# Where w1, w2, one scratch quarter and the kept keys and values stand in the arena of a two-layer decode kernel

## The chip, the core and the metric

The kernel runs on one core of one Trainium2 chip. The metric is device microseconds of that core, from one launch that does everything. A core has a matrix engine (PE, with its weight loads shown apart as PEld), a vector engine (DVE), an activation engine (ACT), a general one (POOL) and SyncE (SP), which here does nothing but start transfers from memory. Sixteen DMA engines carry them.

## The reference

One token of 512 numbers goes through attention and MLP, and then through the same attention and the same MLP once more, with the same weights and the same caches:

```python
def _A_ref(x, k_cache, v_cache, wq, wo):     # x is 1x1x512, H = 32 heads of 128, 4096 cached positions
    q = (x @ wq).reshape(B, Sq, H, Dh) ...
    scores = einsum("bhqd,bhkd->bhqk", q, k_cache) * Dh ** -0.5
    o = einsum("bhqk,bhkd->bhqd", softmax(scores), v_cache)
    return o.reshape(B, Sq, H * Dh) @ wo
def _B_ref(x, w1, b1, w2, b2):               # F = 1376
    return gelu(x @ w1 + b1) @ w2 + b2
x = x + _A_ref(_layernorm(x), ...)
x = x + _B_ref(_layernorm(x), ...)
x = x + _A_ref(_layernorm(x), ...)
x = x + _B_ref(_layernorm(x), ...)
```

Everything is float32. Each cache is 67 MB, so each pass of attention has 134 MB to read.

## The kernel before

**Groups and quarters.** The 32 heads are taken in 8 groups of 4. A group's keys are one load of 8.39 MB (128 partitions of 16384 numbers), its values another. The unit of room is a quarter, U = 512 numbers in each partition (0.26 MB); 32 quarters hold one K or one V. For a group, 32 products with K give the scores in PSUM bank pS (`scores`, L190), `exponentials` (L195) writes the weights p into a scratch quarter of SBUF with an activation, four transposing products (`weights`, L206) bring p into the form that the 32 products with V want (`values`, L220, bank pO), and `head_out` (L225) turns the sum into a scratch quarter, reduces it to o and multiplies it with wo. The next group's query comes after that (`next_queries`).

**The arena.** SBUF is one tile of 109 quarters, and all loads go to fixed places in it. Three homes of 32 quarters stand one behind the other: A from 0, C from 32, B from 64 to 96. K and V of the groups go round in the order A, B, C (`RING`), so that in the first pass B receives V of group 0, K of group 2, V of group 3, K of group 5 and V of group 6 (called V0, K2, V3, K5, V6 below). From 101 stands PAIR, 8 quarters for a pair of weights wo and wq (2.1 MB). Between them the kernel has rooms with names: `SHARED` from 90 (10 quarters, behind the 26 of V6 that stay in B), and `SCRATCH`, the one quarter at 100, which is written twice in each group: by the activation with p, and by `head_out`.

**The second pass** takes the groups in the reverse order, n = 0 to 7 for groups 7 to 0. It finds K7 and V7 still in C and A, and V6 kept: 26 quarters in B and 6 in the PSUM banks pK, copied there by ACT and copied back later. From n = 2 on it loads again, K and V into A, C, B in turn: K(3), V(4), K(6) and V(7) go to B. V(2) is loaded in two pieces of 5 and 3 chunks (a chunk is 4 quarters), as C comes free.

**The change of layers.** Between the passes w1 (4 pieces of 2.69 quarters) and w2 (11 quarters) come through SHARED and the scratch quarter: w1 whole first, then w2 in four pieces into the room of the pieces of w1 that have been used, then wq and the first quarters of K6. Wide products with zeros (`idle`, L154) are put in between; they compute nothing that is used.

**What sets the order.** Each engine takes its instructions in the order in which the program wrote them, and `keep_in_program_order` holds loads and products to it. The framework gives an instruction a wait for every earlier one that reads or writes the same part of a tile. All loads are issued by SP (L70), in one queue: a load that waits holds those behind it. Loads of K and V are written into the program as far ahead as the homes allow.

Of the kernel before, what the change touches and what calls it, by code (L numbers as in the profile page):

```python
# [33 lines left out]


RING = (0, 16 * NC, 8 * NC)
A_AT, B_AT, C_AT = RING
KEPT_V = 26 * U
SHARED = B_AT + KEPT_V
SCRATCH = SHARED + 10 * U  # L40
PAIR = SHARED + 11 * U
ARENA = PAIR + 2 * NC
HALVES = ((0, 4), (4, 8))
W1_AT_END = ((0, 2), (2, 3), (3, 4))
LAST = ((0, 4), (4, 6), (6, 7), (7, 8))
W2_AT_CHANGE = ((0, 2), (2, 5), (5, 8), (8, 11))
W2_AT_END = ((0, 4), (4, 8), (8, 10), (10, 11))
# [3 lines left out]
def decode_layers(ctx: ExitStack, tc: tile.TileContext, x, k, v, w, w1, b1, w2, b2, out):  # L51
# [102 lines left out]
    def idle(to, n=U):  # L154
        matmul(to[:, :n], zero[:, 0:1].to_broadcast([P, P]), at(C_AT, n), start=True, stop=True)

    def minus_mean(s, at):
        for j in range(J):
            matmul(at[32 * j : 32 * j + 32, :], negmean, s, start=True, stop=True)
        return at  # L160

    def mean_of(xs, s):
        nm = minus_mean(s, pS[:, 0:1])
# [6 lines left out]
    def rstd_of(ss):  # L170
        nv = minus_mean(ss, pS[:, 1:2])
        ve, r = small("ve"), small("rstd")
        nc.vector.tensor_scalar(ve, nv, -1.0, EPS, op0=ALU.mult, op1=ALU.add)
        nc.vector.memset(pS[:, 0:2], 0.0)
        nc.gpsimd.tensor_tensor(r, ve, power, op=ALU.pow)
        return r
# [47 lines left out]

    def head_out(rl, wt, last=False):  # L225
        ot = at(SCRATCH, U)
        nc.vector.transpose(ot, pO)  # L227
        o, on = small("o", 4), on_wide
        own = at(SCRATCH, 4 * 129).rearrange("p (b q) -> p b q", q=129)[:, :, :P]
        own = own.rearrange("p b (d q) -> p d b q", q=32)[:, :, :, 0]  # L230
        nc.vector.tensor_reduce(o, own, axis=AX.X, op=ALU.add)  # L231
# [12 lines left out]
        return of_32(turned(pS) if last else turned(pO, wide=True), 4)  # L244

    def mlp(xs, s, w1_t, w2_t, load_w2=None):
        xb = small("xb", 4)
        nc.gpsimd.tensor_tensor(xb, pairs(xs)[:, :, 0], b2c, op=ALU.add)  # L248
        for c in range(4):
            for j in range(J):  # L250
                matmul(pO[32 * j : 32 * j + 2, :FJ], pairs(xs)[:, c, :], w1_t[c][:, FJ * j : FJ * (j + 1)],
                       start=(c == 0), stop=(c == 3))
# [60 lines left out]
    def add_up(acc, own):  # L313
        t = small("acc", 4)
        nc.vector.scalar_tensor_tensor(t, own, 1.0, acc, op0=ALU.mult, op1=ALU.add)
        return t


    negm, z, sc, nsc = first_queries(xs, s, wq_t)
    acc = pairs(xs)[:, :, 0]  # L320
    for g in range(G):
        final = g == G - 1
        k_home, v_home = RING[2 * g % 3], RING[(2 * g + 1) % 3]
        for c, t in blocks(k, g, k_home, HALVES if final else ((0, C),)):
            scores(z, c, t)
        pt, rl = weights(exponentials(sc, nsc))
        for c, t in blocks(v, g, v_home, LAST if final else ((0, C),)):
            values(c, pt, t, c)
            if final and c > 4:
                idle(pS)  # L330
            if g == G - 2:
                for j in range(J):
                    i = 4 * c + j - KEPT_V // U
                    if i >= 0:
                        nc.scalar.copy(pK[i], t[j])
        if final:
            wo_t = by_four(load(PAIR, of_w(g % 2, g, 1)))
            for i in range(3):
                load_w1(SHARED, i, i + 1)
            own = head_out(rl, wo_t, last=True)  # L340
            load_w1(SHARED, 3, 4)
        else:
            pair = load(PAIR, of_w(g % 2, g, 2))
            acc = add_up(acc, head_out(rl, by_four(pair[:, :NC])))
            wq_t = by_four(pair[:, NC:])
            z = next_queries(g + 1, xs, negm, wq_t)
    x1, s1 = set_x(own, 1.0, acc, queries=False)
    own, xb = mlp(x1, s1, in_rows(SHARED, W1C, 4), in_rows(SHARED, U, FB),
                  lambda i: load_w2(SHARED, *W2_AT_CHANGE[i]))
    xs, s = set_x(own, 0.5, xb)  # L350
# [6 lines left out]
    acc = pairs(xs)[:, :, 0]  # L357
    wq_t = by_four(load(SHARED, of_w((g + 1) % 2, g, 1)))
    k_t = []
# [5 lines left out]

    begin_k(SHARED + NC, 4)
    begin_k(SHARED + 2 * NC, 2)
    begin_k(PAIR + NC, 4)
    for c in range(C):
# [12 lines left out]

    v_t = [at(B_AT + U * i, U) for i in range(KEPT_V // U)]
    for i, first in enumerate([C_AT + 30 * U, C_AT + 31 * U] + [PAIR + U * j for j in range(4)]):
        t = at(first, U)
        nc.scalar.copy(t, pK[i])
        v_t.append(t)
    for c in range(C):
# [8 lines left out]
    for n in range(2, G):  # L397
# [67 lines left out]
```

## Time and profile before

| | before |
|---|---|
| median of 3 runs | 680.82 us (680.7 to 681.85) |
| the profiled execution | 679.55 us |
| its span, first to last instruction | 677.8 us |
| busy: PE, DVE, ACT | 433.1, 110.7, 22.2 us |
| granted TensorE clock, mean | 0.841 |
| read from HBM | 286.14 MB, 422 GB/s over the span |
| loads of SP, share of 16 DMA engines' span | 98.7% |

Times in the profile are microseconds from the span's start. A row of the timeline gives start, length, engine, line, operation, tiles, how many instructions were merged, and in brackets the idle time of the engine ahead of it with what ended it. Durations below are from this one execution; its time is 1.27 us under the median of the runs.

### The profile page before, as it was taken

To read this page: it belongs to the slowest core of one execution; us is meant where nothing else is said; L and a number is where in the kernel's file an instruction comes from. 1 tells how busy PE (TensorE), PEld (TensorE's weight loads), DVE (VectorE), ACT (ScalarE), POOL (GpSimd) and SP (SyncE) were. 2 spreads that over 40 slices of the span, in tenths; PEclk is the share of its full clock that TensorE was granted. 3 is DMA by queue.
4 is the path that set the end of the run, shared out by engine and by line. 5 is a ranking of instruction groups with operands and counts; after the bars stand their busy time and mean duration, and the time that the engine had idled before them with its cause. 6 is when DMAs were issued, how large, how long until landed. Compare 5 with 4: busy or idle time off the path is not lost. (4 is left out here: it accounts for less than half of the span.)

```text
span 677.8 us, 6359 instructions
## 1 busy us (share of the span) xinstructions
PE 433.1 (64%) x2792; PEld 119.4 (18%) x2792; DVE 110.7 (16%) x431; ACT 22.2 (3%) x47; POOL 4.3 (1%) x21
## 2 busy tenths in 40 slices
PE   1547666485554874667777897686455764766776
PEld 0112112121111211111113222221111111211112
DVE  1012101111021101210212312211021011210211
ACT  0010000000000000001000110000000000000000
POOL 1000000000000000000000000000000000000000
PEclk9969768797698876977979998998698776977977
DMA  9999999999999999999999999899999999999997
GB/s 372 434 433 433 435 433 433 416 449 437 430 433 413 451 433 430 433 431 422 428 413 359 426 459 414 358 468 441 427 433 398 465 433 423 437 430 410 426 416 294
DMA packets 11404, 286.56 MB, mean 423 GB/s; under 512 B 1776, under 2 KB 1776, under 8 KB 3440
## 3 DMA queue, kind: packets, MB, share of 16 engines
q1 hardware_dynamic: 10944, 286.14, 98.7%
q8 instruction: 22, 0.36, 0.2%
q10 hardware_dynamic: 432, 0.01, 0.0%
q14 instruction: 6, 0.05, 0.0%
HBM read 286.14 MB, written 0.00 MB: 422 GB/s over the span
## 5 line engine op out<-in xcount | busy, mean ns | idle before, releaser
L74 PE MATMUL pO<-arena,turned 128*4 128x512 f32 x1024 | 144.8, 726 | 76.8 <-DMA arena<-in_v 75.6
L74 PE MATMUL pS<-arena,zq 128*8 128x512 f32 x1024 | 137.7, 698 | 70.8 <-DMA arena<-in_k 65.4
L74 PE MATMUL pO<-arena,x_wide 128*128 128x512 f32 (+1 forms) x176 | 54.9, 508 | 24.4 <-DVE turned L137 18.1
L74 PE MATMUL pO<-arena,on_wide 128*128 128x512 f32 x112 | 51.8, 605 | 18.6 <-DVE on_wide L235 18.6
L74 PEld LDWEIGHTS pS<-arena,zq 128*8 128x8 f32 x1024 | 29.1, 99 | 176.3 <-issue 167.1
L74 PEld LDWEIGHTS pO<-arena,turned 128*4 128x4 f32 x1024 | 27.6, 97 | 183.8 <-issue 179.5
L137 DVE STREAM_TRANSPOSE turned<-pO 32x128 f32<-32x128 f32 x112 | 35.0, 312 | 101.1 <-PE pO L74 99.9
L227 DVE STREAM_TRANSPOSE arena<-pO 128x512 f32<-128x512 f32 x16 | 11.5, 717 | 220.4 <-PE pO L74 220.4
L208 PE MATMUL pO<-ident,arena 128*128 128x128 f32 x64 | 14.5, 368 | 43.9 <-ACT arena L203 42.4
L196 DVE TENSOR_REDUCE ml<-pS 128x1 f32<-128x512 f32 x16 | 11.1, 692 | 185.0 <-PE pS L74 185.0
L74 PEld LDWEIGHTS pO<-arena,x_wide 128*128 128x128 f32 (+1 forms) x176 | 21.6, 155 | 57.1 <-DVE turned L137 26.5
L203 ACT ACTIVATE arena<-pS,mt,sc 128x512 f32<-128x512 f32 x16 | 12.4, 777 | 523.7 <-DVE mt L201 523.7
L74 PEld LDWEIGHTS pO<-arena,on_wide 128*128 128x128 f32 x112 | 20.1, 189 | 51.7 <-DVE on_wide L235 31.6
L208 PEld LDWEIGHTS pO<-ident,arena 128*128 128x128 f32 x64 | 9.3, 181 | 58.6 <-ACT arena L203 51.3
L74 PE MATMUL pO<-arena,x 128*2 128x344 f32 x64 | 7.2, 531 | 5.0 <-DMA arena<-in_w 4.4
L74 PE MATMUL pS<-arena,zero 128*128 128x512 f32 x16 | 9.9, 706 | 0.0
L74 PE MATMUL pS<-arena,gelu_g 128*1 128x128 f32 x176 | 6.7, 290 | 1.5 <-DVE gelu_g L270 1.3
L213 DVE STREAM_TRANSPOSE mt<-ml 128x32 f32<-128x32 f32 x16 | 3.4, 212 | 17.2 <-ACT arena L203 17.2
L74 PEld LDWEIGHTS pS<-arena,gelu_g 128*1 128x1 f32 x176 | 3.9, 88 | 7.4 <-DVE gelu_g L270 3.7
L211 DVE COPY turned<-pO 128x128 f32<-128x128 f32 x16 | 4.4, 277 | 3.1 <-PE pO L208 3.1
L74 PE MATMUL pO<-arena,zero 128*128 128x512 f32 x8 | 4.5, 644 | 0.0
L248 POOL TENSOR_TENSOR xb<-x,b2c 128x4 f32<-128x4 f32 x2 | 0.4, 200 | 636.9 <-DVE x L148 636.9
(71 smaller groups left out, 76.5 us busy)
## 6 DMA issues: line engine op xcount, KB each, us to landing
arena<-in_w SPq DMA_DIRECT2D x13, 2048.0 KB, 28.8
arena<-in_k SPq DMA_DIRECT2D x4, 4096.0 KB, 42.5
arena<-in_v SPq DMA_DIRECT2D x2, 4096.0 KB, 47.6
arena<-in_w SPq DMA_DIRECT2D x6, 1024.0 KB, 20.3
arena<-in_v SPq DMA_DIRECT2D x1, 5120.0 KB, 23.8
arena<-in_w SPq DMA_DIRECT2D x6, 688.0 KB, 30.2
arena<-in_v SPq DMA_DIRECT2D x2, 2048.0 KB, 50.8
arena<-in_v SPq DMA_DIRECT2D x4, 1024.0 KB, 53.3
```

The costliest lines, as they stand in the source:

```text
L74: tc.keep_in_program_order(nc.tensor.matmul(*a, **kw))
L137: nc.vector.transpose(t[q], src[q, P * j : P * (j + 1)])
L196: nc.vector.tensor_reduce(ml[:, 0:1], pS, axis=AX.X, op=ALU.max)
L203: nc.scalar.activation(p, pS, AF.Exp, bias=bias[:, 0:1], scale=sc, accum_out=ml[:, 0:1])
L208: tc.keep_in_program_order(nc.tensor.transpose(pT[:, b].rearrange("p j r -> p (j r)"), p[:, P * b : P * (b + 1)], ident))
L211: nc.vector.tensor_copy(pt, pT[:, :, :, :C].rearrange("p b j c -> p j c b"))
L213: nc.vector.transpose(lt, ml)
L227: nc.vector.transpose(ot, pO)
L248: nc.gpsimd.tensor_tensor(xb, pairs(xs)[:, :, 0], b2c, op=ALU.add)
```

## The change

Constants first. V6 keeps 27 quarters in B and 5 in PSUM, and the PSUM bank that this frees takes the last quarter of K6, so the second pass reads 31 quarters of K6 instead of 32. SHARED begins at 91 and has 10 quarters. SCRATCH is moved from quarter 100 into that room: SHARED + 4 quarters, which is quarter 95. The last head output of the first pass has a place of its own (LAST_OT). w1's fourth piece goes into the first one's room once that is used, and w2 comes in five pieces (1, 2, 4, 3, 1 quarters).

In the MLP the products with w1 go to pS and the mean and variance to pO (before: the other way round), and idle products stand at other places. V(2) is loaded as 6 and 2 chunks.

```diff
 RING = (0, 16 * NC, 8 * NC)
 A_AT, B_AT, C_AT = RING
-KEPT_V = 26 * U
-SHARED = B_AT + KEPT_V
-SCRATCH = SHARED + 10 * U
-PAIR = SHARED + 11 * U
+KEPT_V, KEPT_K = 27, 1
+SHARED = B_AT + KEPT_V * U
+SCRATCH = SHARED + 4 * U
+LAST_OT = SHARED + 3 * W1C
+PAIR = SHARED + 10 * U
 ARENA = PAIR + 2 * NC
-W2_AT_CHANGE = ((0, 2), (2, 5), (5, 8), (8, 11))
+W1_AT_CHANGE = (0, W1C, 2 * W1C, 0)
+W2_AT_CHANGE = ((0, 1, 9 * U), (1, 3, 3 * U), (3, 7, 5 * U), (7, 10, 0), (10, 11, 3 * U))
...
+    def idle_beside(to, first):
+        matmul(to[:, first:], zero[:, 0:1].to_broadcast([P, P]), at(C_AT, U - first), start=False,
+               stop=False, skip_group_check=True)
...
-    def mlp(xs, s, w1_t, w2_t, load_w2=None):
+    def mlp(xs, s, w1_t, w2_t, load_w1=None, load_w2=None):
...
             if c == 0:
-                nm, ss = mean_of(xs, s)
+                nm, ss = mean_of(xs, s, pO)
+                if load_w1:
+                    load_w1(3)
             if c == 1:
-                r = rstd_of(ss)
-            if load_w2 and c < 3:
+                r = rstd_of(ss, pO)
+            if load_w2 and 0 < c < 3:
                 load_w2(c)
-        idle(pS)
-        ht = at(SCRATCH, 32 * FB)
-        nc.vector.transpose(ht, pO[:, : 32 * FB])
+                idle_beside(pS, 32 * FB)
+        ht = at(SHARED, 32 * FB)
+        nc.vector.transpose(ht, pS[:, : 32 * FB])
...
         if load_w2:
             load_w2(3)
+        idle(pS)
...
-            if load_w2 and any(c == b - 1 for a, b in W2_AT_CHANGE):
-                idle(pO)
+            if load_w2 and c == 1:
+                load_w2(4)
+            if load_w2 and c in (2, 6, 9, 10):
+                idle(pO, U if c < 4 else U // 2)
...
+        if g == G - 2:
+            for i in range(KEPT_K):
+                nc.scalar.copy(pK[4 * C - KEPT_V + i], t[J - KEPT_K + i])
...
-            for i in range(3):
-                load_w1(SHARED, i, i + 1)
-            own = head_out(rl, wo_t, last=True)
-            load_w1(SHARED, 3, 4)
+            for c in range(3):
+                w1_at_change(c)
+            own = head_out(rl, wo_t, last=True, place=LAST_OT)
+            w2_at_change(0)
+            idle(pO, U // 2)
...
-    begin_k(SHARED + NC, 4)
-    begin_k(SHARED + 2 * NC, 2)
+    begin_k(SHARED, 4)
+    begin_k(SHARED + 9 * U, 1)
     begin_k(PAIR + NC, 4)
...
-    pair = load(C_AT + 22 * U, of_w(g % 2, g - 1, 2))
+    pair = load(C_AT + 6 * NC, of_w(g % 2, g - 1, 2))
...
-        for c, t in blocks(v, g, v_home, LAST if final else ((0, 5), (5, 8)) if n == 2 else ((0, C),)):
+        for c, t in blocks(v, g, v_home, LAST if final else ((0, 6), (6, 8)) if n == 2 else ((0, C),)):
```

On SP's queue the loads of K and V stand in the same order as before. What each load waits for is not the same. The first loads of the first pass, before (K0, V0 into B, the first pair, K1, V1, the next pair, K2 into B; a name in brackets is a semaphore of the engine or of an earlier load):

```order
L70 DMA arena<-in_k 128x16384
L70 DMA arena<-in_v 128x16384 [waits DMAHW1_49,PE_49]
L70 DMA arena<-in_w 128x4096
L70 DMA arena<-in_k 128x16384
L70 DMA arena<-in_v 128x16384 [waits DMAHW4_49,DMAHW0_49,PE_49]
L70 DMA arena<-in_w 128x4096 [waits DMAHW6_49,PE_49]
L70 DMA arena<-in_k 128x16384 [waits DMAHW5_49,DMAHW2_49]
```

and the same loads after the change:

```order
L75 DMA arena<-in_k 128x16384
L75 DMA arena<-in_v 128x16384 [waits DMAHW1_49,PE_49,Activation_49]
L75 DMA arena<-in_w 128x4096
L75 DMA arena<-in_k 128x16384
L75 DMA arena<-in_v 128x16384 [waits DMAHW4_49,DMAHW0_49]
L75 DMA arena<-in_w 128x4096 [waits DMAHW6_49,PE_49]
L75 DMA arena<-in_k 128x16384 [waits DMAHW2_49,DMAHW5_49,DVE_49,PE_49]
```

V0 has a wait for ACT that it did not have, and K2 waits for DVE and PE that it did not have; V1, which goes to A, has lost its own wait for PE, which the one ahead of it in the queue now covers.

In the second pass, from the pair that precedes K(3): before,

```order
L70 DMA arena<-in_w 128x4096 [waits DMAHW3_49,Activation_49]
L70 DMA arena<-in_k 128x16384
L70 DMA arena<-in_v 128x16384 [waits DMAHW0_49,PE_49]
L70 DMA arena<-in_w 128x4096 [waits DMAHW3_49,PE_49]
L70 DMA arena<-in_k 128x16384 [waits DMAHW2_49,DMAHW1_49]
L70 DMA arena<-in_v 128x16384 [waits DMAHW4_49,PE_49]
```

and after the change:

```order
L75 DMA arena<-in_w 128x4096 [waits DMAHW4_49,Activation_49]
L75 DMA arena<-in_k 128x16384 [waits DVE_49,PE_49]
L75 DMA arena<-in_v 128x16384 [waits DMAHW1_49]
L75 DMA arena<-in_w 128x4096 [waits DMAHW4_49,PE_49]
L75 DMA arena<-in_k 128x16384 [waits DMAHW3_49,DMAHW2_49]
L75 DMA arena<-in_v 128x16384 [waits DMAHW5_49,PE_49,Activation_49]
```

K(3), the second row, had no wait at all and now waits for DVE and PE; V(4), the last row, waits for ACT besides.

More of the change, by code (lines that the diff above doesn't have):

```diff
@@ L160, in minus_mean, with mean_of @@
         return at
-    def mean_of(xs, s):
-        nm = minus_mean(s, pS[:, 0:1])
+    def mean_of(xs, s, bank=pS):
+        nm = minus_mean(s, bank[:, 0:1])
         xc, sq, ss, negm = small("xc", 4), small("sq", 4), small("ss"), small("negm")
@@ L168, in mean_of, with rstd_of @@
         return negm, ss
-    def rstd_of(ss):
-        nv = minus_mean(ss, pS[:, 1:2])
+    def rstd_of(ss, bank=pS):
+        nv = minus_mean(ss, bank[:, 1:2])
         ve, r = small("ve"), small("rstd")
         nc.vector.tensor_scalar(ve, nv, -1.0, EPS, op0=ALU.mult, op1=ALU.add)
-        nc.vector.memset(pS[:, 0:2], 0.0)
+        if bank is pS:
+            nc.vector.memset(pS[:, 0:2], 0.0)
         nc.gpsimd.tensor_tensor(r, ve, power, op=ALU.pow)
@@ L223, in values, with head_out @@
                    start=(i == 0), stop=(i == C - 1))
-    def head_out(rl, wt, last=False):
-        ot = at(SCRATCH, U)
+    def head_out(rl, wt, last=False, place=SCRATCH):
+        ot = at(place, U)
         nc.vector.transpose(ot, pO)
         o, on = small("o", 4), on_wide
-        own = at(SCRATCH, 4 * 129).rearrange("p (b q) -> p b q", q=129)[:, :, :P]
+        own = at(place, 4 * 129).rearrange("p (b q) -> p b q", q=129)[:, :, :P]
         own = own.rearrange("p b (d q) -> p d b q", q=32)[:, :, :, 0]
@@ L316, in add_up, with w1_at_change, w2_at_change @@
         return t
+    def w1_at_change(c):
+        load(SHARED + W1_AT_CHANGE[c], w1[:, W1C * c : W1C * (c + 1)])
+    def w2_at_change(i):
+        a, b, first = W2_AT_CHANGE[i]
+        load(SHARED + first, w2[:, U * a : U * b])
     negm, z, sc, nsc = first_queries(xs, s, wq_t)
@@ L332, in decode_layers @@
                 for j in range(J):
-                    i = 4 * c + j - KEPT_V // U
+                    i = 4 * c + j - KEPT_V
                     if i >= 0:
@@ L347, in decode_layers @@
     x1, s1 = set_x(own, 1.0, acc, queries=False)
-    own, xb = mlp(x1, s1, in_rows(SHARED, W1C, 4), in_rows(SHARED, U, FB),
-                  lambda i: load_w2(SHARED, *W2_AT_CHANGE[i]))
+    own, xb = mlp(x1, s1, [at(SHARED + first, W1C) for first in W1_AT_CHANGE],
+                  [at(SHARED + first + U * i, U) for a, b, first in W2_AT_CHANGE for i in range(b - a)],
+                  w1_at_change, w2_at_change)
     xs, s = set_x(own, 0.5, xb)
@@ L357, in decode_layers @@
     acc = pairs(xs)[:, :, 0]
-    wq_t = by_four(load(SHARED, of_w((g + 1) % 2, g, 1)))
+    wq_t = by_four(load(SHARED + 5 * U, of_w((g + 1) % 2, g, 1)))
     k_t = []
@@ L364, in begin_k, with back @@
         k_t.extend(at(home + U * i, U) for i in range(n))
-    begin_k(SHARED + NC, 4)
-    begin_k(SHARED + 2 * NC, 2)
+    def back(i, first):
+        t = at(first, U)
+        nc.scalar.copy(t, pK[i])
+        return t
+    begin_k(SHARED, 4)
+    begin_k(SHARED + 9 * U, 1)
     begin_k(PAIR + NC, 4)
@@ L374, in decode_layers @@
             begin_k(C_AT + 2 * NC, 14)
-    pair = load(C_AT + 22 * U, of_w(g % 2, g - 1, 2))
+            k_t.append(back(5, C_AT + 22 * U))
+    pair = load(C_AT + 6 * NC, of_w(g % 2, g - 1, 2))
     p = exponentials(sc, nsc)
@@ L381, in decode_layers @@
     acc = add_up(acc, head_out(rl, wo_t))
[L383 to L387, printed above, removed]
+    v_t = [at(B_AT + U * i, U) for i in range(KEPT_V)]
+    v_t += [back(i, C_AT + 23 * U if i == 0 else PAIR + U * (i - 1)) for i in range(4 * C - KEPT_V)]
     for c in range(C):
```

2 lines of the change are left out of this document (1 added, 1 removed).

## The prediction

> **What bounds the kernel now.** I read the page first, then the busy times by stretch, then SP's own timeline.
>
> ```profile
> HBM read 286.14 MB, written 0.00 MB: 422 GB/s over the span
> ```
>
> ```profile
> 8.00:340.00 332.00, 197.55 (x1119) 52.80 (x1112) 49.10 (x181) 11.41 (x23) 0.55 (x1) 0.82 1.00 430
> 356.00:375.00 19.00, 14.68 (x239) 6.13 (x242) 4.72 (x30) 0.21 (x1) 1.74 (x6) 1.00 0.96 358
> 427.00:432.00 5.00, 3.36 (x20) 0.84 (x23) 1.48 (x5) 0.00 (x0) 0.00 (x0) 1.00 0.63 202
> 432.00:672.00 240.00, 157.18 (x968) 41.97 (x964) 39.45 (x149) 5.42 (x13) 0.75 (x2) 0.82 1.00 430
> ```
>
> The last three numbers of a stretch are the granted TensorE clock, the share of the DMA engines, and GB/s. The transfers run at 430 GB/s with a DMA share of 1.00 outside the change of layers, while PE is busy 60 to 65% of the time: the kernel is bound by the queue of loads, and any time in which that queue is empty is lost for good. It is short of loads at two places only: 356 to 375 (358 of 430 GB/s, 3.2 us lost) and 427 to 432 (202 of 430, 2.7 us lost). At 430 GB/s a K or a V (8.39 MB) takes 19.5 us, and one with a pair of weights ahead of it (10.49 MB) 24.4 us.
>
> Why the queue is never empty elsewhere is seen in when SP issues the loads that go to home B:
>
> ```profile
> 8.35 0.33 SPq L70 DMA_DIRECT2D arena<-in_v  x1
> 66.28 0.38 SPq L70 DMA_DIRECT2D arena<-in_k  x1
> 123.78 0.33 SPq L70 DMA_DIRECT2D arena<-in_v  x1
> 196.60 0.42 SPq L70 DMA_DIRECT2D arena<-in_k  x1
> 254.20 0.33 SPq L70 DMA_DIRECT2D arena<-in_v  x1
> 429.65 0.43 SPq L70 DMA_DIRECT2D arena<-in_k  x1
> 473.12 0.33 SPq L70 DMA_DIRECT2D arena<-in_v  x1
> 547.47 0.42 SPq L70 DMA_DIRECT2D arena<-in_k  x1
> ```
>
> They are V0, K2, V3, K5, V6 and, in the second pass, K(3), V(4), K(6). V0 leaves at 8.35, while K0 is still being carried; the others too leave while one or two large loads are ahead of them. That a load which waits holds those behind it is seen at V(2) and K(3); SP's waits, and its timeline with the two pieces of V(2) as one row:
>
> ```profile
> SPq L70 <- PE pO L74: 209.4, 16, 22.0
> ```
>
> ```profile
> 406.36 22.77 SPq L70 DMA_DIRECT2D arena<-in_v  x2
> ```
>
> The second piece was issued at the end of that row, at 428.80 (an issue takes 0.33), after SP's longest wait for PE, 22.0 us. K(3) had nothing of its own to wait for and still left only at 429.65, right behind it.
>
> **The change part by part.**
>
> *The scratch quarter.* B is quarters 64 to 96. SCRATCH goes from quarter 100 to SHARED + 4, which is 91 + 4 = 95: the last quarter of B. The activation writes p there in every group and `head_out` writes its sum there. So each load into B now shares a quarter with the scratch, and the order of the program makes it wait for the last reader of what was written there. For V of a group that reader is the four transposes of the same group's p, and p comes from the scores of K, the load just ahead of V. For K it is the reduction to o of the group before, at the end of that group's V. The rows of SP show it: ACT's wait appears at V0 and V(4), DVE's at K2 and K(3), and so for all eight. Everything else goes on as it did. V(7) also goes to B, but in four pieces, of which only the last touches quarter 95; its 7.34 MB ahead take 17 us, more than the 12 to 15 us below, so it costs nothing, as long as those three pieces are queued.
>
> Eight times, then, the queue runs dry. The waits are measured from these bursts in the timeline: scores and transposes ahead of the four V, and the products with V ahead of the K:
>
> ```profile
> 25.39 9.65 PE L74 MATMUL pS<-arena,zq 128*8 128x512 f32 x64 [17.05 <-DMA arena<-in_k]
> 39.16 1.08 PE L208 MATMUL pO<-ident,arena 128*128 128x128 f32 x4 [4.11 <-ACT arena L203]
> 46.12 9.52 PE L74 MATMUL pO<-arena,turned 128*4 128x512 f32 x64 [5.88 <-DMA arena<-in_v]
> 157.91 9.95 PE L74 MATMUL pS<-arena,zq 128*8 128x512 f32 x64 [5.85 <-DMA arena<-in_k]
> 170.60 1.12 PE L208 MATMUL pO<-ident,arena 128*128 128x128 f32 x4 [2.74 <-ACT arena L203]
> 288.73 9.40 PE L74 MATMUL pS<-arena,zq 128*8 128x512 f32 x64 [4.56 <-DMA arena<-in_k]
> 300.86 1.12 PE L208 MATMUL pO<-ident,arena 128*128 128x128 f32 x4 [2.74 <-ACT arena L203]
> 508.09 8.95 PE L74 MATMUL pS<-arena,zq 128*8 128x512 f32 x64 [5.01 <-DMA arena<-in_k]
> 519.77 0.66 PE L208 MATMUL pO<-ident,arena 128*128 128x128 f32 x4 [2.74 <-ACT arena L203]
> 89.75 9.89 PE L74 MATMUL pO<-arena,turned 128*4 128x512 f32 x64 [6.18 <-DMA arena<-in_v]
> 220.86 9.20 PE L74 MATMUL pO<-arena,turned 128*4 128x512 f32 x64 [7.32 <-DMA arena<-in_v]
> 571.05 9.88 PE L74 MATMUL pO<-arena,turned 128*4 128x512 f32 x64 [6.18 <-DMA arena<-in_v]
> ```
>
> ```profile
> 100.47 0.18 DVE L231 TENSOR_REDUCE o<-arena 128x4 f32<-128x16 f32 x1
> ```
>
> From the landing of K (start of the scores) to the end of the transposes: 25.39 to 40.24 = 14.9 us for V0, 157.91 to 171.72 = 13.8 for V3, 288.73 to 301.98 = 13.3 for V6, 508.09 to 520.43 = 12.3 for V(4). From the landing of V to the end of o: 89.75 to 100.65, that is the products and 1.0 us.
>
> *Starting again.* A load that finds the queue empty pays what a load in a full queue does not. Three landings show it, in the view of DMA issues (the last number is us from issue to landing), beside the issue of wq:
>
> ```profile
> arena<-in_v SPq DMA_DIRECT2D x1, 3072.0 KB, 9.8
> arena<-in_k SPq DMA_DIRECT2D x1, 34.7
> arena<-in_k SPq DMA_DIRECT2D x1, 24.1
> ```
>
> ```profile
> 0.74 0.38 SPq L70 DMA_DIRECT2D arena<-in_w  x1
> ```
>
> The first is the piece of V(2) issued at 428.80 into an empty queue: 3.15 MB is 7.3 us, it took 9.8, so 2.5 over. The second is K(3), issued at 429.65, with that piece and a pair ahead of it: landing at 464.35, 35.55 us after 428.80 for 13.63 MB, or 31.7 us: 3.9 over. The third is K0, issued at 1.18 behind 1.05 MB of wq that left at 0.74: 24.5 us for 9.44 MB (21.9), 2.6 over. So the excess is larger the more is loaded after the start. Here 27 to 38 MB follow each start before the next wait, more than in the second row; I take that row's 3.9, with 2.5 as the low end. To this comes 0.1 us from the release to SP's issue.
>
> The Trainium skill, DMA: Bandwidth & Descriptors, section on the anatomy of one DMA, gives a fixed cost of about 2.0 us for a transfer, most of it the receipt of the last byte. By that figure, an estimate, the eight starts would cost 8 x 1.9 = 15 us less and the time would be 774. The rows above have 2.5 to 3.9, and the measurement decides.
>
> *The sum.* A V in B lands later by its wait + 0.1 + 3.9, since it had followed K without a gap: 17.8 for V3, 17.3 for V6, 16.3 for V(4). For V0: 40.24 + 0.1 + 19.5 + 3.9 = 63.7 instead of 46.12, 17.6. Together 69.0. A K in B had come 24.4 us after the V ahead, behind a pair; now it comes the products + 1.0 + 0.1 + 19.5 + 3.9 after it, so it is later by the products + 0.1: 10.0 for K2, 9.3 for K5, 10.0 for K(6), together 29.3. Between these, the loads behind a late one are released at once and follow in the old rhythm, so the delays add.
>
> *The change of layers, V(2) and K(3).* From 384 to 460 the chain of waits runs over PE and DVE alone, so here a load counts only if it becomes late for PE. Two of its rows, then PE's and SP's timeline:
>
> ```profile
> 430.35 7.10 PE pS L74 x64
> ...
> 450.46 0.19 DVE o L231
> ```
>
> ```profile
> 362.18 0.76 PE L74 MATMUL pO<-arena,x 128*2 128x344 f32 x8 [0.93 <-DMA arena<-in_w]
> 365.62 1.12 PE L74 MATMUL pO<-arena,zero 128*128 128x512 f32 x2
> 410.19 8.40 PE L74 MATMUL pO<-arena,turned 128*4 128x512 f32 x64 [0.38 <-DVE turned L211]
> 441.55 8.09 PE L74 MATMUL pO<-arena,turned 128*4 128x512 f32 x64 [0.38 <-DVE turned L211]
> 464.49 8.56 PE L74 MATMUL pS<-arena,zq 128*8 128x512 f32 x64 [4.74 <-DMA arena<-in_k]
> ```
>
> ```profile
> 358.84 1.14 SPq L70 DMA_DIRECT2D arena<-in_w  x2
> ```
>
> w1's fourth piece must now wait for the first products with w1, as the first of the loads at 358.84 did before: 0.7 MB (1.6 us) with 2.5 to start lands at 363.0, against 362.18 when its products ran, 0.8 later. In return three wide idle products of 1.12 us between the chunks of w2 (365.62 is one) become one wide and two half ones, 1.1 less, if w2's five pieces come in time. Ends: 1 us gained, 1.5 lost; I take 0. The half idle product in x1's chain (0.6 us) stands where PE waits for DVE to turn `own` and make x1, and the two of 160 columns where it waits for w1; without that cover they would be 1.3 us together.
>
> V(2)'s first piece, now 6 chunks, takes room in which a quarter of V6 stands, so it waits for the seventh chunk of those products, 410.19 + 7/8 of 8.40 = 417.5, instead of leaving at 406. It lands at 417.5 + 0.1 + 14.6 + 3.9 = 436.1, and its products start at 441.55: hidden, with 5 us of cover. The 0.26 MB of K6 that are not read are 0.6 us of transfer in a stretch that PE sets: 0. K(3) waits for o, 450.65: + 0.1 + 19.5 + 3.9 = 474.2 against 464.49, 9.7 us.
>
> Total 69.0 + 29.3 + 9.7 = 108.0 us on 679.55 us, the profiled execution: 787.5. The median of the runs is 1.27 above it: **788.8 us**.
>
> **The rivals.**
>
> *The queue covers the waits* (not slower). If each load into B were released before the loads ahead of it are through, nothing would be lost, and 0.6 us of K6 and up to 2.7 us of the gap at 427 would be gained: 677.6. It would hold from the point at which 13 us x 430 GB/s = 5.6 MB stand in the queue between K and V. For it speaks that two large loads are queued now. Against it: V is the very next load after the K whose scores it waits for, so the queue is empty by construction when K has landed.
>
> *K costs nothing.* If the pair and what else is in the queue covered the end of `head_out`, only the four V would be paid: 680.82 + 69.0 = 750. The pair covers 4.9 us of 10.9; it would have to be twice as large.
>
> *Cold bursts.* PE now stands idle over 20 us ahead of some bursts, not 5 to 7. The 64 products at 430.35 took 7.1 us; at half that clock they would take 14.2, and the 9.0 to 9.95 above are a mixture. If all bursts on which a load waits, but the one at 441.55, ran slow to their end, 7 x 4.6 = 32 us more: 821. Against it: the scores at 25.39 came after 17.05 us of idling and took 9.65, like the rest. The Trainium skill, TensorE: Matmul & The Clock Gate, Part 1, says that the clock falls to half after an idle window of 3.4 us and is released by one such window of work; by that rule these bursts start cold already, and longer idling adds nothing.
>
> **How the numbers follow.** The forecast has a chance of 0.84, K at no cost 0.06, cold bursts 0.05, cover 0.03, the rest 0.02. Low end of the forecast's range: starts at 2.5 us (8 x 1.4 = 11 less) and waits all of the shortest kind (3 to 4 less): 774. High end: waits of V as for V0 (2 more each at three), bursts of 9.95 all, 1.5 us at w1, and bursts up to 1 us colder: 803. The range leaves the first two rivals and most of the third out, 0.14 in all. What a measurement of this kernel can tell from no change is about 0.2%, 1.4 us; faster 0.02, same 0.01, slower 0.97.
>
> **What would show it.** In the new profile: V0 issued near 40, not 8.35; K2 near 118 (89.75 + 17.6 + 10.9); eight stretches of some 8 to 17 us in the row of DMA shares that fall far under 9; SP's longest waits on PE's transposes and on DVE's o; HBM's mean near 364 GB/s; PE's and DVE's busy time much as before. It is wrong if V0 still leaves ahead of the scores of K0, if a K in B lands in the old rhythm, or if the bursts lengthen beyond 10 us.

## The result, and the profile after

The changed kernel takes 787.41 us (median of 6 executions, 783.23 to 790.92), the kernel before 680.76 us on the same chip: a ratio of 1.156, with a 95% interval of 1.152 to 1.160. The forecast was 788.8 us. Rows of the profile of after (its execution took 787.05 us): the span, the row of DMA shares and the GB/s in forty slices of 19.6 us, and the mean.

```profile
span 785.3 us, 6374 instructions
...
DMA  9299959992999599928999999969982999699997
GB/s 394 88 384 454 435 224 427 425 428 110 417 435 427 218 424 428 427 111 374 401 429 397 347 447 381 395 265 427 428 374 107 440 449 409 253 427 425 434 421 296
...
HBM read 285.88 MB, written 0.00 MB: 364 GB/s over the span
```

Eight slices read 2, 5 or 6 among slices of 9; two of the slices of 8 lie beside a 2 and belong to the same gaps, and the 7 is the end of the kernel. The 2 belong to V0, V3, V6 and V(4), the 5 and 6 to K2, K5, K(3) and K(6). SP's own rows for the loads into home B, with their start:

```profile
40.22 0.33 SPq L75 DMA_DIRECT2D arena<-in_v  x1
117.88 0.33 SPq L75 DMA_DIRECT2D arena<-in_k  x1
196.72 0.33 SPq L75 DMA_DIRECT2D arena<-in_v  x1
275.04 0.33 SPq L75 DMA_DIRECT2D arena<-in_k  x1
356.08 0.33 SPq L75 DMA_DIRECT2D arena<-in_v  x1
522.00 0.33 SPq L75 DMA_DIRECT2D arena<-in_k  x1
602.24 0.33 SPq L75 DMA_DIRECT2D arena<-in_v  x1
678.88 0.33 SPq L75 DMA_DIRECT2D arena<-in_k  x1
```

V0 leaves at 40.22 (8.35 before) and K2 at 117.88 (66.28 before). What they wait for, in SP's waits (in total, how often, the longest):

```profile
SPq L75 <- PE pO L219: 308.2, 6, 71.1
...
SPq L75 <- DVE o L242: 127.5, 4, 37.0
```

L219 are the transposes of p, L242 is the reduction to o. Before, SP's waits have no row for the transposes, and for o one wait of 23.3 us. A wait on SP costs nothing by itself, since SP used to wait too; what it costs is seen in what the DMA engines do meanwhile. The stretches from the landing of the load ahead to the release of V0, K2, V3 and K5, in the view of stretches (length, then the busy time and instructions of PE, PEld, DVE, ACT and POOL, the granted clock, the DMA share, GB/s):

```profile
25.20:40.20 15.00, 10.82 (x68) 2.68 (x68) 2.46 (x11) 2.15 (x3) 0.00 (x0) 0.91 0.00 1
107.00:117.90 10.90, 9.79 (x64) 1.82 (x64) 0.95 (x3) 0.00 (x0) 0.00 (x0) 0.74 0.26 113
184.80:196.70 11.90, 9.10 (x68) 2.21 (x68) 2.13 (x9) 0.87 (x2) 0.00 (x0) 0.88 0.00 0
264.30:275.00 10.70, 9.63 (x64) 1.83 (x64) 0.90 (x2) 0.00 (x0) 0.00 (x0) 0.75 0.19 81
```

In front of a V nothing at all is carried; in front of a K only what is left of the pair.

How late the kernel becomes is read by setting the same bursts of PE side by side. (The 32 products of a burst in the program are 64 rows in the profile, x64.) After:

```profile
62.78 9.71 PE L79 MATMUL pO<-arena,turned 128*4 128x512 f32 x64 [22.65 <-DMA arena<-in_v]
87.19 9.46 PE L79 MATMUL pS<-arena,zq 128*8 128x512 f32 x64 [4.52 <-DMA arena<-in_k]
107.01 9.79 PE L79 MATMUL pO<-arena,turned 128*4 128x512 f32 x64 [6.51 <-DMA arena<-in_v]
184.81 8.45 PE L79 MATMUL pS<-arena,zq 128*8 128x512 f32 x64 [5.66 <-DMA arena<-in_k]
219.19 8.32 PE L79 MATMUL pO<-arena,turned 128*4 128x512 f32 x64 [22.53 <-DMA arena<-in_v]
245.00 9.07 PE L79 MATMUL pS<-arena,zq 128*8 128x512 f32 x64 [7.37 <-DMA arena<-in_k]
317.97 8.43 PE L79 MATMUL pO<-arena,turned 128*4 128x512 f32 x64 [8.65 <-DMA arena<-in_v]
377.96 9.15 PE L79 MATMUL pO<-arena,turned 128*4 128x512 f32 x64 [21.94 <-DMA arena<-in_v]
588.78 9.55 PE L79 MATMUL pS<-arena,zq 128*8 128x512 f32 x64 [6.45 <-DMA arena<-in_k]
649.88 9.71 PE L79 MATMUL pS<-arena,zq 128*8 128x512 f32 x64 [6.43 <-DMA arena<-in_k]
721.50 9.74 PE L79 MATMUL pO<-arena,turned 128*4 128x512 f32 x64 [6.69 <-DMA arena<-in_v]
```

and the rows of before that the prediction did not show:

```profile
177.26 8.81 PE L74 MATMUL pO<-arena,turned 128*4 128x512 f32 x64 [5.55 <-DMA arena<-in_v]
201.51 8.64 PE L74 MATMUL pS<-arena,zq 128*8 128x512 f32 x64 [5.33 <-DMA arena<-in_k]
264.49 9.57 PE L74 MATMUL pO<-arena,turned 128*4 128x512 f32 x64 [6.97 <-DMA arena<-in_v]
308.23 9.88 PE L74 MATMUL pO<-arena,turned 128*4 128x512 f32 x64 [6.25 <-DMA arena<-in_v]
374.11 7.05 PE L74 MATMUL pS<-arena,zq 128*8 128x512 f32 x64 [0.48 <-DVE pS L174]
551.70 9.33 PE L74 MATMUL pS<-arena,zq 128*8 128x512 f32 x64 [4.64 <-DMA arena<-in_k]
614.66 8.57 PE L74 MATMUL pO<-arena,turned 128*4 128x512 f32 x64 [5.80 <-DMA arena<-in_v]
```

The start of each burst after less its start before is the delay up to there; the growth between two of them is the price of the load between. A late load is read at a burst behind it, except V6, which is read at its own products, because K7 and V7 behind it come in pieces.

| part | read at the burst | late by | part's price | predicted |
|---|---|---|---|---|
| V0 | 107.01 - 89.75 | 17.26 | 17.3 | 17.6 |
| K2 | 184.81 - 157.91 | 26.90 | 9.6 | 10.0 |
| V3 | 245.00 - 201.51 | 43.49 | 16.6 | 17.8 |
| K5 | 317.97 - 264.49 | 53.48 | 10.0 | 9.3 |
| V6 | 377.96 - 308.23 | 69.73 | 16.2 | 17.3 |
| change of layers | 444.99 - 374.11 | 70.88 | 1.2 | 0 |
| K(3) | 588.78 - 508.09 | 80.69 | 9.8 | 9.7 |
| V(4) | 649.88 - 551.70 | 98.18 | 17.5 | 16.3 |
| K(6) | 721.50 - 614.66 | 106.84 | 8.7 | 10.0 |
| the rest | spans, 785.3 - 677.8 | 107.5 | 0.7 | 0 |

(444.99 is the start of the scores of the second pass, quoted below.) So the four V cost 67.6 us together, K2, K5 and K(6) 28.3, K(3) 9.8. The 0.7 in the last row belongs to K(6): the products with V(7) start at 756.30 instead of 648.69, 107.61 late, and from there on nothing more is lost. V(7) itself costs nothing, as forecast: the last eight of its products, at 767.01, wait for no load.

### The profile page after: what moved, and what is told of

It is laid out like the page before. It is cut to its first block, busy times and chain, and to the rows that moved or that the text cites. A ratio compares the mean times of both kernels' runs of the same rounds, so it can differ in the third digit from the quotient of the medians.

```text
span 785.3 us, 6374 instructions
## 1 busy us (share of the span) xinstructions
PE 427.2 (54%) x2798; PEld 119.3 (15%) x2798; DVE 110.3 (14%) x429; ACT 22.3 (3%) x47; POOL 4.3 (1%) x21
## 4 chain that ended last, share of the span: by engine, by line
DMA 57%; PE 30%; another core or an unknown queue 5%; DVE 5%; issue 1%; ACT 1%; SPq 1%; ACTq 0%; DVEq 0%
DMA arena<-in_v 25%; DMA arena<-in_k 24%; PE pO L79 16%; PE pS L79 13%; DMA arena<-in_w 8%; ACT arena L214 1%; PE pO L219 1%; DVE turned L142 1%; DVE arena L238 1%; DVE ml L207 1%; SPq L75 1%; DVE mb L211 0%; DVE mt L212 0%; DVE mt L209 0%
## 5 line engine op out<-in xcount | busy, mean ns | idle before, releaser
L79 PE MATMUL pO<-arena,turned 128*4 128x512 f32 x1024 | 142.0, 714 | 146.6 <-DMA arena<-in_v 145.4
L79 PE MATMUL pO<-arena,on_wide 128*128 128x512 f32 x112 | 51.8, 605 | 18.7 <-DVE on_wide L246 18.7
L219 PE MATMUL pO<-ident,arena 128*128 128x128 f32 x64 | 13.7, 350 | 43.9 <-ACT arena L214 42.3
L219 PEld LDWEIGHTS pO<-ident,arena 128*128 128x128 f32 x64 | 8.8, 173 | 58.5 <-ACT arena L214 51.2
L79 PE MATMUL pS<-arena,zero 128*128 128x512 f32 (+1 forms) x20 | 10.1, 586 | 1.3 <-DVE arena L274 1.3
L79 PE MATMUL pS<-arena,x 128*2 128x344 f32 x64 | 6.0, 451 | 4.6 <-DMA arena<-in_w 4.6
L224 DVE STREAM_TRANSPOSE mt<-ml 128x32 f32<-128x32 f32 x16 | 3.4, 211 | 17.2 <-ACT arena L214 17.2
L79 PEld LDWEIGHTS pS<-arena,zero 128*128 128x128 f32 x20 | 3.0, 187 | 8.4 <-issue 5.8
```

What stands on the lines that cost most here:

```text
L79: tc.keep_in_program_order(nc.tensor.matmul(*a, **kw))
L219: tc.keep_in_program_order(nc.tensor.transpose(pT[:, b].rearrange("p j r -> p (j r)"), p[:, P * b : P * (b + 1)], ident))
L224: nc.vector.transpose(lt, ml)
```

## Experiments

Each time stands beside the kernel before on the same chip. It took 681.11 us where the scratch at 100, the scratch at 95 in the kernel before, the next K ahead and V(2) in three pieces ran, 680.19 for the two halves of the scratch, the wide idle products and the three pieces in the kernel before, and 680.91 for the new order of w1 and w2.

**The scratch back at quarter 100, all the rest of the change kept.** The theory is that the scratch quarter makes the whole loss; the rival that some of it lies in the new order at the change of layers.

```diff
-SCRATCH = SHARED + 4 * U
+SCRATCH = SHARED + 9 * U
...
-    begin_k(SHARED + 9 * U, 1)
+    begin_k(SHARED + 4 * U, 1)
```

> The changed kernel with one thing undone: SCRATCH is quarter 100 (SHARED + 9) instead of 95, and the single early quarter of K6 takes 95 in exchange. No load into B shares a quarter with the scratch then. Theory (all of the loss is the shared quarter): about 682 us, 681 to 683, a ratio to before of 1.000 to 1.003; the small rest is the 1.3 us by which the changed kernel was late over the change of layers. V0 leaves near 8 again. Rival (the order of w1 and w2, the idle products and the 6 and 2 chunks cost a good part of the 107 us, and the shared quarter only makes it worse): over 690.

Measured: 683.03 us (12 executions), ratio 1.0026 [1.0006, 1.0046]. 104.4 of the 106.6 us are gone with this edit, and in the row of DMA shares all gaps with them:

```profile
DMA  9999999999999999999998998999999999999997
```

What remains of the change costs 1.9 us. In its one profile 0.64 us of that are there when the second pass opens (scores at 374.75 against 374.11), and 1.73 at the scores with K(3) (466.22 against 464.49). The four kernels at the end of this section look for it.

**The kernel before with its scratch at quarter 95.** The converse: no other part of the change (the few things that would overwrite each other there, the last head output, the turned MLP row and the early quarters of K6, are given other quarters).

```diff
-SCRATCH = SHARED + 10 * U
+SCRATCH = SHARED + 5 * U
+LATE = SHARED + 10 * U
...
-        ot = at(SCRATCH, U)
+        place = LATE if last else SCRATCH
+        ot = at(place, U)
...
-    begin_k(SHARED + NC, 4)
-    begin_k(SHARED + 2 * NC, 2)
+    begin_k(SHARED + 6 * U, 4)
+    begin_k(SHARED + 4 * U, 1)
+    begin_k(LATE, 1)
```

> The kernel before with only the scratch moved into B: p and the head sums go to quarter 95 (the last head sum of the first pass and the MLP's transposed sum stay at 100, and the early quarters of K6 are loaded around 95). Nothing else of the change. Theory: the same eight loads wait, 680.8 + 106 = 787, 780 to 793. Rival (w1 and w2 in another order, or the idle products, are part of the loss): clearly less, under 770.

Measured: 785.12 us (2 executions), ratio 1.152 [1.151, 1.154]. SP's waits are those of after, with the line numbers of this kernel:

```profile
SPq L71 <- PE pO L209: 308.4, 6, 71.0
SPq L71 <- DVE o L233: 124.9, 4, 35.3
```

Taking the place away takes the loss away, and adding it to the kernel before adds the loss.

**p alone, in the first pass alone.** The scratch at 100, but the activation writes p at quarter 95 for groups 0 to 6 of the first pass. Only V0, V3 and V6 should be late. (The edit that puts the scratch at 100, as in the first experiment, is also in the next kernel and in the two with three pieces built on the changed kernel; it is not shown in full again.)

```diff
-SCRATCH = SHARED + 4 * U
+SCRATCH = SHARED + 9 * U
...
-    def exponentials(sc, nsc):
+    def exponentials(sc, nsc, place=SCRATCH):
...
-        p = at(SCRATCH, U)
+        p = at(place, U)
...
-        pt, rl = weights(exponentials(sc, nsc))
+        pt, rl = weights(exponentials(sc, nsc, SCRATCH if final else SHARED + 4 * U))
```

> The kernel with SCRATCH at quarter 100, except that p stands in quarter 95 in groups 0 to 6 of the first pass; the head sums stay at 100. V0, V3 and V6 wait for the transposes of p as in the changed kernel, K2 and K5 wait for nothing late. Theory (eight delays that add, each with its own wait): 683 + 17.3 + 16.6 + 16.2 = 733, 729 to 737. Rival (the delays of V and K in one round hang together, so that with V late the work behind it is late anyway): the full delay of the first pass without the K, or with them, comes out nearer 700 or 750.

Measured: 732.97 us in one execution, 49.9 above the kernel with the scratch at 100, which ran on another chip; against the kernel before on each chip it is 50.9. The three V of the table have 50.1.

```profile
SPq L75 <- PE pO L219: 198.5, 5, 61.4
...
SPq L75 <- DVE o L242: 24.0, 1, 24.0
```

The waits for the transposes are there, those for o are not (the one that is left is there with the scratch at 100 too, 23.5 us).

**The head sums alone, in the first pass alone.** The same for what `head_out` writes; only K2 and K5 should be late. By the rival "K costs nothing" the pair would cover it.

```diff
-            acc = add_up(acc, head_out(rl, by_four(pair[:, :NC])))
+            acc = add_up(acc, head_out(rl, by_four(pair[:, :NC]), place=SHARED + 4 * U))
```

> The kernel with SCRATCH at quarter 100, except that the head sums stand in quarter 95 in groups 0 to 6 of the first pass; p stays at 100. K2 and K5 wait for the reduction to o, V0, V3 and V6 for nothing late. Theory: 683 + 9.7 + 9.7 = 702, 699 to 706. Rival (K in B costs nothing by itself, the pair of weights covers it): 683.

Measured: 700.84 us in one execution, 17.8 above the scratch at 100 (18.7 against the kernel before on each chip), or 8.9 to 9.3 for each K; the rival falls. In SP's waits the picture is the reverse: there is no row for the transposes, and three waits for o.

```profile
SPq L75 <- DVE o L242: 105.7, 3, 42.3
```

The two halves of the cause add up: 49.9 + 17.8 = 67.7 us, or 50.9 + 18.7 = 69.6 by chip, where the first pass of after has 69.7.

**The next K queued ahead of the V that waits.** If the queue runs dry because V is the very next load behind the K it waits for, another load between them must cover a part. In the changed kernel K1 is written ahead of V0 and K4 ahead of V3 (they go to C and A, whose room is free), the data and products are the same.

```diff
+        if g in (1, 4):
+            early = [(c, quarters(k_home + NC * c)) for c in range(C)]
+        else:
+            early = blocks(k, g, k_home, HALVES if final else ((0, C),))
-        for c, t in blocks(k, g, k_home, HALVES if final else ((0, C),)):
+        for c, t in early:
...
+        if g in (0, 3):
+            load(RING[(2 * g + 2) % 3], part(k, g + 1, 0, C))
```

> The changed kernel, with K1 put on the queue ahead of V0 and K4 ahead of V3; the waits are all kept. Three accounts. Delays add and the queue's order is their cause: both of these waits are hidden behind a load of 19.5 us, 16.7 and 15 us less, 755 us. The waits are hidden, but the next load into B waits for the same PE work and takes up half (my theory): V0 lands near 64 as now, but K1 is already there, scores of group 1 end near 95, products with V1 near 108, K2 leaves near 110 instead of 117.9; 8 us gained there and 7 at K5: 772 us, 768 to 777. The order on the queue does not matter: 787.

Measured: 763.04 us in one execution: 24.4 us less than the changed kernel, where 772, 15 less, was expected, and by the two other readings 755 or 787. The direction is right, and part of the cover is given back at the next load into B, as expected; the size is not. K2 and K5 in SP's timeline:

```profile
106.08 0.33 SPq L75 DMA_DIRECT2D arena<-in_k  x1
...
252.47 0.33 SPq L75 DMA_DIRECT2D arena<-in_k  x1
```

They leave 11.8 and 22.6 us earlier than in after. I had them wait for two bursts of about 9.5 us, with the idling that these have in the other kernels. But K1 is now there when V0 lands, so PE comes from V0's products straight to the scores of K1:

```profile
85.73 7.05 PE L79 MATMUL pS<-arena,zq 128*8 128x512 f32 x64 [1.65 <-DVE zq L197]
...
97.00 7.99 PE L79 MATMUL pO<-arena,turned 128*4 128x512 f32 x64 [0.38 <-DVE turned L222]
```

These take 7.05 and 7.99 us, 4.0 less for the two than assumed; the same two bursts of group 4 take 7.05 and 8.34, 3.6 less. That is 7.6 of the 9 us that the expectation lacked.

**The 1.9 us that are left: V(2) in three pieces.** With the scratch at 100, V(2) comes as 5, 1 and 2 chunks instead of 6 and 2, so that most of it need not wait for the seventh chunk of V6's products.

```diff
-        for c, t in blocks(v, g, v_home, LAST if final else ((0, 6), (6, 8)) if n == 2 else ((0, C),)):
+        for c, t in blocks(v, g, v_home, LAST if final else ((0, 5), (5, 6), (6, 8)) if n == 2 else ((0, C),)):
```

> The kernel with SCRATCH at quarter 100, and V(2) in three pieces of 5, 1 and 2 chunks instead of 6 and 2, so that the first leaves after the scores ahead of it (about 407) and the sixth chunk alone waits for the products with V6. Theory (with the scratch out of B, transfers set the pace again from the change of layers on, and the queue does not run dry ahead of V(2)): K(3) lands near 463, 1.4 us earlier than before, 679.4 us, ratio 0.996 to 0.999. Rival (the stretch is set by PE, so a gap in the queue there costs nothing): as with two pieces, 681 to 683.

Measured: 682.58 us (12 executions; one of them took 1473.24 us and is not in the ratio), ratio 1.0020 [1.0008, 1.0033]. The expected 679.4 did not come. V(2)'s first piece did leave earlier, and the queue was not dry ahead of it; but in the profiled execution PE ran the idle products amid w1 and w2 at half its clock:

```profile
364.84 2.08 PE L79 MATMUL pS<-arena,zero 128*128 128x512 f32 x2 [0.65 <-DVE arena L274]
...
368.23 2.08 PE L79 MATMUL pO<-arena,zero 128*128 128x512 f32 x2
```

The first of these takes 1.13 us with V(2) in two pieces. That one profile names a cost of 1.9 us does not show that the other executions had it.

**The same with four wide idle products.** To keep the clock up there, two whole idle products after w1 and whole ones instead of halves amid w2.

```diff
+        if load_w2:
+            idle(pO)
...
-                idle(pO, U if c < 4 else U // 2)
+                idle(pO)
```

> The kernel with SCRATCH at quarter 100 and V(2) as 5, 1 and 2 chunks, with a wide idle product right behind the products with w1 and wide instead of half ones between the chunks of w2. In the profile of the kernel without them the clock was at 0.50 from 364 to 369, in its sibling with 6 and 2 chunks at 1.00. Theory (the clock falls in some executions because PE idles while it waits for w1's late fourth piece, and that costs the 2 us which the third piece should have brought): clock 1.00 at the change of layers, 680.5, ratio 0.997 to 1.000. Rival (the late loads of w1 and w2 cost it, whatever the clock): 682 to 684.

Measured: 681.77 us against 680.19, ratio 1.0025 [1.0013, 1.0037]. The half clock at 364 is not in this profile, and the ratio is no better. So keeping the clock up at that one place did not bring the 1.9 us back; in this profile a stretch of half clock stood later, at 388 to 392.

**The three pieces in the kernel before.** Its queue was dry for 2.7 us at 427 to 432, ahead of the second piece of V(2).

```diff
-    pair = load(C_AT + 22 * U, of_w(g % 2, g - 1, 2))
+    pair = load(C_AT + 24 * U, of_w(g % 2, g - 1, 2))
...
-        for c, t in blocks(v, g, v_home, LAST if final else ((0, 5), (5, 8)) if n == 2 else ((0, C),)):
+        for c, t in blocks(v, g, v_home, LAST if final else ((0, 5), (5, 6), (6, 8)) if n == 2 else ((0, C),)):
```

> The kernel before with V(2) in three pieces of 5, 1 and 2 chunks, the pair ahead of it at C + 24 and the two quarters of V6 that come back at C + 22 and C + 23, so that the sixth chunk can leave after the products with V6 and the queue does not run dry at 427. Nothing else. Theory (K(3) follows on the queue, so a gap of 2.4 us ahead of it is paid): K(3) lands 2 to 2.4 us earlier, 678.6, ratio 0.996 to 0.998. Rival (as with three pieces in the other kernel, where nothing could be measured: PE sets that stretch): 681, ratio 1.000.

Measured: 679.90 us against 680.19, ratio 0.9989 [0.9978, 1.0001]. The interval holds both no gain and the smallest gain expected. SP's row of the three pieces (start of the first to end of the last) and the row of K(3):

```profile
407.92 23.00 SPq L70 DMA_DIRECT2D arena<-in_v  x3
...
431.96 0.47 SPq L70 DMA_DIRECT2D arena<-in_k  x1
```

The queue is no longer empty ahead of the last piece, but K(3) leaves 2.3 us later than before, and its scores start at 465.24 instead of 464.49. This does not show that the gap was worth nothing. The profiled execution is the slowest of the twelve (681.78 us), and in it PE is already late when the last piece waits for it: a burst at 387.14 took 8.75 us instead of 7.05, and the scores at 432.21 start 1.86 later than before. PE still waits 3.63 us for K(3), so the queue does set the end there. What closing the gap is worth in an execution without that loss stays open. This is the only kernel here with a median below that of before, and it can't be told from it.

**The new order of w1 and w2 alone.** In the kernel before, w1's fourth piece goes into the first one's room and w2 comes in five pieces, with the four whole idle products left as they were. The pieces are not those of the change: 2, 2, 3, 3 and 1 quarters instead of 1, 2, 4, 3 and 1, and the first early quarters of K6 come in three loads instead of two.

```diff
-W2_AT_CHANGE = ((0, 2), (2, 5), (5, 8), (8, 11))
+W1_AT_CHANGE = (0, W1C, 2 * W1C, 0)
+W2_AT_CHANGE = ((0, 2, 3 * W1C), (2, 4, 3 * U), (4, 7, 5 * U), (7, 10, 0), (10, 11, 3 * U))
...
-            load_w1(SHARED, 3, 4)
+            w2_at_change(0)
```

> The kernel before with the new order of w1's and w2's pieces alone: the scratch stays at quarter 100, V(2) stays in pieces of 5 and 3 chunks, the four idle products stay as they were. Theory: the 1.9 us that the change cost with its scratch back at quarter 100 (683.03 against 681.1) come from the later landings of w1's last piece and of w2's pieces, so this kernel is 1 to 2 us slower than before, ratio 1.0015 to 1.003. Rival: they come from the kept quarter, from the pieces of V(2) or from the idle products, so this kernel stays at the time before, ratio 0.9995 to 1.0005.

Measured: 684.07 us against 680.91, ratio 1.0047 [1.0031, 1.0063], 3.2 us. The rival falls, and the price is more than I gave. Two rows of its profile:

```profile
363.33 0.76 PE L75 MATMUL pO<-arena,x 128*2 128x344 f32 x8 [2.39 <-DMA arena<-in_w]
...
388.44 8.75 PE L75 MATMUL pO<-arena,turned 128*4 128x512 f32 x64 [0.38 <-DVE turned L212]
```

The products with w1's fourth piece wait 2.39 us for it (0.93 before) and start 1.15 later: this is the theory's cost. The second row took 7.05 us in the kernel before; 1.7 us are a stretch of half clock. The same 8.75 us stand in the profiles of the kernel with three pieces and wide idle products and of the kernel before with three pieces, so they are not bound to this order, and one profile does not tell how often they come. The order of w1 and w2 is shown to cost something between 2.1 and 4.3 us in this surrounding; how it splits in the six executions is open, and so is whether the order of the change, with its other pieces, costs as much (the whole change without its scratch costs 1.9).

## Why the prediction was right

*The mechanism.* Four kernels bear out the chain "shared quarter, wait for transposes or o, SP's queue held, DMA engines without work": the change without it, the kernel before with it, and p and the head sums apart. The signs named ahead stand in the rows above: 40.22 and 117.88 for "near 40" and "near 118", 364 GB/s, the eight slices, SP's two kinds of waits. PE is busy 427.2 us (433.1 before) and DVE 110.3 (110.7), so nothing but waiting was added.

*The sum.* 108.0 us were forecast on the profiled execution and 107.5 came. By kind of load they are within 1.4 us: the V 69.0 against 67.6, three K 29.3 against 28.3, K(3) 9.7 against 9.8. Single loads miss by up to 1.3 us either way, so that the sum came within 0.5 is in part luck: the misses cancel. The V were 0.3 to 1.2 too high in the first pass, 1.2 too low at V(4). At V3 and V(4) this is the wait: it was taken from the bursts of before, and these differ from one execution to the next, 8.45 us for the scores at 184.81 and 9.95 for the same burst before, 9.55 at 588.78 and 8.95 before. V6 had a longer burst than forecast and is low for another reason, the next point.

*Starting again* was taken as 3.9 us for each load, from one row. The first load behind a dry queue has less: V0 left at 40.22 and its products started at 62.78, 22.6 us for 19.5; V3 took 22.5, V6 21.9, V(4) 22.4; that is 2.3 to 3.0 with the 0.1 from the landing to the products taken off. Then it grows. From V0's products to the scores of K1 and on to those with V1 it is 24.41 and 19.82 us, before (scores of K1 at 70.36) 24.24 and 19.39, 0.6 more; behind V3 it is 25.81 against 24.25, 1.6 more; behind V(4) 1.0 more, behind V6, up to the first products with V7, 0.5. Together that is 3.6, 4.4, 3.8 and, for V6, 2.8, where 3.9 was put for all. So the size was about right for three of four. The argument of that step, that the excess is larger the more is loaded after the start, fits the growth of the landings, but they are not all of the story.

The traces keep sixteen landing times for each load, and a load counts as landed at the last of them. In after, the sixteen of K0, the first large load, lie within 0.4 us, those of V0 behind the dry queue within 1.2, those of V1 within 1.8, those of K4 within 2.6. Taken by the mean of the sixteen, V0 is 17.2 us later than before and V1 17.1, V3 and K4 both 42.6, V(4) and the load behind it both 98.1: nothing more is lost after the start. What grows is the lag of the last of the sixteen behind their mean, which was there all along in the kernel before (V3's lie within 2.0).

The sum by the 2.0 us of the Trainium skill (DMA: Bandwidth & Descriptors, the anatomy of one DMA) was 774, 13 us under the result. The page gives that figure for transfers that the general engine starts; here SP starts them.

*K* came out right by two errors that cancel, which is luck. The prediction has the pair, 4.9 us, carried while the products run, which leaves 6.0 of 10.9 us dry. By the stretches above the DMA share from 107.00 to 117.90 is 0.26, which is about 2.8 us of work: some 2.1 of the pair had been carried ahead of V1's last landing. The dry time is about 8.1, and the rest of K2's 9.6 is 1.5 us, where 4.0 was put. What the queue loses is nearly the same sum, but the 3.9 can't be taken as a cost of the empty queue alone.

*The change of layers* was put at 0 with ends of 1 gained and 1.5 lost; 1.2 came. PE's rows:

```profile
429.12 0.76 PE L79 MATMUL pS<-arena,x 128*2 128x344 f32 x8 [0.72 <-DMA arena<-in_w]
430.78 0.76 PE L79 MATMUL pS<-arena,x 128*2 128x344 f32 x8 [0.40 <-DMA arena<-in_w]
...
433.10 0.76 PE L79 MATMUL pS<-arena,x 128*2 128x344 f32 x8 [1.09 <-DMA arena<-in_w]
...
438.44 1.05 PE L79 MATMUL pS<-arena,gelu_g 128*1 128x128 f32 x32 [0.55 <-DMA arena<-in_w]
...
440.59 0.84 PE L79 MATMUL pS<-arena,gelu_g 128*1 128x128 f32 x24 [0.46 <-DMA arena<-in_w]
...
444.99 7.05 PE L79 MATMUL pS<-arena,zq 128*8 128x512 f32 x64 [0.48 <-DVE pS L185]
```

From the third to the fourth products with w1 it is 2.32 us, before 1.68: the 0.8 of the prediction measured 0.64. The 1.1 us to be saved by narrower idle products are not there, because the condition put to them, "if w2's five pieces come in time", did not hold: PE waits 0.55 and 0.46 us for pieces of w2. And the second products with w1, at 429.12, wait 0.72 us for their piece, which they did not do before. The prediction has no such term; in the scratch at 100 that wait is absent and in the kernel before with three pieces it is 0.56, so it comes and goes without the change. This step failed, by 1.2 us in 107.5.

*V(2)* was said to be hidden with 5 us of cover. It left at 489.08, which is 418.2 without the 70.9 us of delay (417.5 forecast), and its products did not wait for it:

```profile
489.08 11.23 SPq L75 DMA_DIRECT2D arena<-in_v  x2
```

```profile
512.45 8.46 PE L79 MATMUL pO<-arena,turned 128*4 128x512 f32 x64 [0.42 <-DVE turned L222]
```

*The rivals.* "The queue covers the waits" and "K costs nothing" fall with the rows of DMA shares and with the head sums alone. "Cold bursts" falls too: after 22.65, 22.53 and 21.94 us of idling the products took 9.71, 8.32 and 9.15, before 9.52, 8.81 and 9.88 after some 6. The rule of the Trainium skill (TensorE: Matmul & The Clock Gate, Part 1) that the clock is down already after one idle window agrees with this, and with the 7.05 us after 1.65 of idling in the experiment with the next K ahead.

## What to carry to other kernels

Where one queue carries all loads in order, the place of a small scratch tile is part of the schedule: a quarter of 0.26 MB that overlaps the room of a later load ties that load to the scratch's last reader, and the load behind cannot pass it. Ask of each load what it shares memory with, who reads that last, and what is still in the queue at that time; the loss is the time from the landing of the last load ahead to the release, plus the restart (2.8 to 4.4 us here for a load of 8.39 MB), less what else the queue still carries, and such losses add up when every load after it follows in its rhythm.

A gap in the queue that is seen in one profile is not yet a gain: closing the 2.7 us at 427 brought nothing that the runs tell from no change, and the one profile of it had lost 1.7 us elsewhere, so what the gap is worth was not found out.

## What was not expected of the hardware

Starting an empty queue again showed up in two parts: 2.3 to 3.0 us at the first load, and 0.5 to 1.6 more at the loads behind it. The second part is no loss of work. The sixteen landing times of a load lie within 0.4 us at K0 and within 1.8 to 2.6 at loads well behind a restart, a load counts as landed with the last of them, and by the mean of the sixteen the delay behind a restart stays the same to 0.1 us. Why they come apart is not shown.

64 products that stood waiting 4 us or more for a load took 8.3 to 10 us in the rows above, and 7.05 and 7.99 when 1.65 and 0.38 us of idling lay ahead: a change in the order of loads moved PE's time by 4 us in two bursts. A short idle alone does not give the short time: 8.46 and 8.75 us stand after 0.42 and 0.38 us at 512.45 and 388.44 above, and the burst at 387.27 in the kernel before took 7.05 after the same 0.39. And stretches of half clock come at different places in kernels that hardly differ (364 to 369 in one, about 388 to 393 in three others, neither in the change with its scratch at 100); they are worth 1.7 to 1.9 us each, as much as the last parts of this change.
